# Attention value products in quarters of the matmul array, and first pairs loaded in runs of four tokens

## The chip, the cores and the metric

The kernel runs on one core of one Trainium2 chip. The metric is device time in microseconds (us). Before the change three runs took 802.65, 802.65 and 802.79 us; the median is 802.65.

## What is computed

Normalised attention on 8 batches, 12 heads, 448 tokens, 64 channels a head, and then a feed-forward block on the 3584 x 768 result:

```python
q_n, k_n = (rmsnorm(q, g_q), rmsnorm(k, g_k))
scores = scale * np.matmul(q_n, k_n.transpose(0, 1, 3, 2))
scores = scores - np.max(scores, axis=-1, keepdims=True)
attn = np.exp(scores)
attn = attn / (np.sum(attn, axis=-1, keepdims=True) + 1e-09)
attn_out = np.matmul(attn, v)
...
h = x @ w_in                      # 768 -> 1024
e = np.exp(h - np.max(h, axis=-1, keepdims=True))
solu = h * (e / (np.sum(e, axis=-1, keepdims=True) + 1e-09))
ln = (solu - mu) / np.sqrt(var + 1e-06) * g_ln
out = ln @ w_out                  # 1024 -> 768
```

## The kernel before

fast_path does all of it in three stages that follow each other on TensorE. general_path is another way for unusual inputs, and isn't run here.

**Attention.** The 96 heads are done four at a time: a "quad" m, 0 to 23, holds two "pairs" a = 2m and b = 2m + 1 of two heads each. A pair's normalised q and k lie transposed in a tile qkT, head h on partitions 64h to 64h + 63. `scores` (L812) multiplies 64 keys of one head at a time, so four matmuls use the four quarters (64 x 64) of the array, and writes one tile s of two PSUM banks; ScalarE takes the exponential (L802) into a tile E. Of 448 keys, three such units of 128 keys belong to each pair, and the last 64 keys of both pairs share a unit (`scores_last`, L825). A quad thus has seven score units. `values_last` (L858) starts the output o of both pairs from the last keys, in quarters; `values(a)` and `values(b)` (L869) add the other keys with all 128 rows and half the columns of the array. `sums` (L891) adds E over the keys with a matrix of ones, 32 columns at a time. `inverse` and `divide` (L902 to L918) turn the sums into factors and multiply o by them into xo; `store_x` (L926) puts xo into a scratch tensor xd in HBM.

The next quads are prepared alongside: `load` (L636), `squares` on ScalarE (L672), `row_sums` on VectorE (L680), `fold_sums` on Pool (L690, L691), `rsqrt_seed` on ScalarE (L697, L698, result ny), `normalise` on Pool (L713), `qk_transpose` on VectorE (L723) and `gain` on ScalarE (L727). `add` (L839) and `add_more` (L848) add E tiles into es ahead of the sums. In twelve quads, w_in is also converted from 64-bit words: `begin` and `step` on ScalarE and VectorE (L535 to L542), `combine_in` on Pool (L563).

The order of all this is written out by hand: the tile framework's scheduler is off (`tc.manual_schedule()`), every engine runs its instructions in the order in which the loop over m emits them, and the framework adds the waits for data and for buffers that come free. `unit(f)` emits a piece of TensorE's work and counts its steps; `later(n, f)` emits f after n more units. In the loop, a quad emits scores(a, 0), store_x(m - 1), the other score units with the preparation between them, then squares, gains and sums, then `outputs` (values_last and values(a)), the weight conversion, values(b), and the sums.

The first two pairs take another way: `load_rows` (L738) loads them with tokens on partitions, `square_rows`, `sum_rows` and `normalise_rows` (L772) work on rows, `transpose_rows` (L778) transposes q (s = 0) and k (s = 1) on TensorE into PSUM tiles pt, and `take_rows` (L784 to L788) copies these to qkT, on ScalarE for pair 0, on ScalarE and VectorE for pair 1.

**Hidden layer.** For each of 14 groups of 256 tokens `products` (L990) makes x @ w_in out of seven block products into PSUM banks A, B, C, D. `load_x` (L942) brings a group from xd; `sizes` (L951) squares it on ScalarE for a check at the end of the program; `block_sums` (L970 to L974) makes the sums of blocks on Pool; `plus` (L1006) adds a bank to an earlier part on VectorE. **Output.** `outer_product` (L1205) does the same for the second matrix.

## Time and profile before

The page shown is of one profiled execution. That execution took 803.36 us; the span from its first to its last instruction is 801.6 us.

| | |
|---|---|
| profiled execution | 803.36 us |
| its span | 801.6 us |
| median of the runs | 802.65 us |
| TensorE busy (PE) | 788.1 us, 98% |
| VectorE (DVE) | 613.7 us, 77% |
| Pool | 523.1 us, 65% |
| ScalarE (ACT) | 472.2 us, 59% |
| L812 scores / L869 values | 120.1 us / 113.8 us of TensorE |
| granted TensorE clock | 0.999 |

By stretch TensorE is busy 7.0 of the first 10.6 us, 21.9 of the next 22.9, all of 33.5 to 296.7, 18.6 of the 19.6 us to 316.3, and all of 316.3 to 560.

How to read the lines below. A timeline line has the start in us, the length, the engine, the line of the kernel, the operation, output and inputs, how many instructions were merged, and in brackets how long the engine sat idle before and what ended that. PE is TensorE's matmul; each fp32 matmul is two records (passes), so L869's 24 are 12 matmuls. Matmuls are pipelined: one begins before the one ahead has ended, and the spacing of the starts tells what one costs. A form such as 64*64 is the part of the array that is used, rows by columns. A line of the chain of waits has the start, the length, and the engine and line that the end of the program hung on at that time; "issue" is time without a visible cause.

### The profile page before, as it was taken

How to read it: one execution, taken by the hardware profiler on the slowest of the kernel's cores; microseconds unless marked ns; L12 is line 12 of the kernel's file. 1: busy time of each engine (PE TensorE's matmuls, PEld its weight loads, DVE VectorE, ACT ScalarE, POOL GpSimd, SP SyncE). 2: the span in 40 equal slices, each digit the busy share in tenths (PEclk: the TensorE clock that was granted, in tenths of full speed). 3: DMA queues.
4: the chain of work that ended last, by engine and by line, in shares of the span. 5: the costliest groups of instructions: out<-in, count | busy, mean ns of one | idle time of the engine just before them, and what ended most of it. 6: DMA issues, size and time to landing. Idle time of an engine off the chain costs nothing.

```text
span 801.6 us, 14271 instructions
## 1 busy us (share of the span) xinstructions
PE 788.1 (98%) x4854; PEld 462.7 (58%) x4854; DVE 613.7 (77%) x1202; ACT 472.2 (59%) x783; POOL 523.1 (65%) x664
## 2 busy tenths in 40 slices
PE   8999999999999999999999999999999999999997
PEld 4344444444444443444444444444789999999996
DVE  6787989989888896488878666777896776866945
ACT  6677878878778774376766544444515455464420
POOL 2666777778876784234456467668698777877861
PEclk9999999999999999999999999999999999999999
DMA  9878889897787832445554435552757457366312
GB/s 169 164 174 156 175 194 186 194 189 161 169 157 169 158 102 75 136 117 155 152 146 131 113 98 141 142 137 52 190 167 233 147 183 264 123 221 223 112 61 83
DMA packets 269598, 122.68 MB, mean 153 GB/s; under 512 B 187596, under 2 KB 254668, under 8 KB 269516
## 3 DMA queue, kind: packets, MB, share of 16 engines
q1 hardware_dynamic: 254332, 111.78, 55.9%
q10 hardware_dynamic: 15184, 9.90, 4.5%
q8 instruction: 40, 0.66, 0.3%
q14 instruction: 42, 0.34, 0.1%
HBM read 84.94 MB, written 36.70 MB: 152 GB/s over the span
## 4 chain that ended last, share of the span: by engine, by line
PE 87%; DVE 3%; DMA 2%; SPq 2%; POOL 2%; ACT 2%; issue 1%; DVEq 0%; ACTq 0%; POOLq 0%
PE A L1205 14%; PE A L990 13%; PE o L869 12%; PE s L812 12%; PE B L990 8%; PE B L1205 7%; PE C L990 4%; PE sm L891 4%; PE D L990 4%; PE C L1205 3%; PE s L825 2%; PE o L858 2%; SPq L636 1%; DMA xg<-xd 1%; ACT E L802 1%
## 5 line engine op out<-in xcount | busy, mean ns | idle before, releaser
L802 ACT ACTIVATE E<-s 128x896 f32<-128x896 f32 x168 | 138.8, 937 | 8.3 <-PE s L812 7.8
L812 PE MATMUL s<-qkT 64*64 64x448 f32 x1152 | 120.1, 545 | 1.0 <-ACT qkT L786 0.6
L869 PE MATMUL o<-E,v 128*64 128x448 f32 x576 | 113.8, 543 | 0.0
L1079 POOL TENSOR_TENSOR he<-he,mhalf 128x1 f32<-128x1 f32 x28 | 27.4, 977 | 102.5 <-DVE he L1078 97.4
L812 PEld LDWEIGHTS s<-qkT 64*64 64x64 f32 x1152 | 48.0, 163 | 59.4 <-ACT E L802 29.3
L1205 PE MATMUL A<-w_out,sums 128*128 128x192 f32 x392 | 79.9, 327 | 1.6 <-POOL sums L1185 1.2
L869 PEld LDWEIGHTS o<-E,v 128*64 128x64 f32 x576 | 39.1, 137 | 72.2 <-issue 68.0
L1205 PE MATMUL B<-w_out,sums 128*128 128x192 f32 x392 | 79.8, 326 | 0.5 <-DVE P L1267 0.5
L713 POOL TENSOR_TENSOR qkn<-qk,ny 128x896 f32<-128x896 f32 x46 | 77.2, 1699 | 3.8 <-DMA qk<-in_q_dram 1.5
L848 POOL TENSOR_TENSOR es<-es,E 128x896 f32<-128x896 f32 x22 | 46.4, 2110 | 48.8 <-ACT sq L672 34.0
L990 PE MATMUL B<-w_in,xsum 128*128 128x512 f32 x168 | 76.7, 592 | 0.0
L990 PE MATMUL A<-w_in,xg 128*128 128x512 f32 x168 | 74.6, 593 | 0.0
L1061 ACT ACTIVATE u<-h,hmax 128x1024 f32<-128x1024 f32 x28 | 32.2, 1148 | 66.8 <-DVE hmax L1055 66.8
L1205 PEld LDWEIGHTS A<-w_out,sums 128*128 128x128 f32 x392 | 66.1, 190 | 2.4 <-POOL sums L1185 1.5
L1205 PEld LDWEIGHTS B<-w_out,sums 128*128 128x128 f32 x392 | 66.2, 190 | 0.8 <-DVE P L1267 0.8
L839 DVE TENSOR_TENSOR es<-E 128x896 f32<-128x896 f32 x48 | 53.9, 1124 | 2.7 <-ACT E L802 2.7
L990 PEld LDWEIGHTS B<-w_in,xsum 128*128 128x128 f32 x168 | 31.9, 190 | 40.2 <-issue 39.2
L990 PEld LDWEIGHTS A<-w_in,xg 128*128 128x128 f32 x168 | 31.8, 190 | 40.1 <-issue 39.3
L690 POOL COPY ss<-part 32x56 f32<-32x56 f32 x92 | 47.0, 511 | 5.9 <-DVE part L680 1.4
L680 DVE TENSOR_REDUCE part<-sq 128x28 f32<-128x896 f32 x46 | 47.9, 1080 | 3.9 <-ACT sq L672 1.6
L723 DVE STREAM_TRANSPOSE qkT<-qkn 128x896 f32<-128x896 f32 x46 | 48.4, 1087 | 0.0
L563 POOL TENSOR_TENSOR w_out<-w_out 128x384 f32<-128x384 f32 x44 | 45.0, 1028 | 1.3
(153 smaller groups left out, 1651.0 us busy)
## 6 DMA issues: line engine op xcount, KB each, us to landing
ur<-ud SPq DMA_DIRECT2D x60, 256.0 KB, 4.6
ud<-ub SPq DMA_DIRECT2D x112, 128.0 KB, 2.3
xd<-xo SPq DMA_DIRECT2D x48, 224.0 KB, 3.0
qk<-in_q_dram SPq DMA_DIRECT2D x92, 112.0 KB, 3.1
qk<-in_k_dram SPq DMA_DIRECT2D x92, 112.0 KB, 3.0
v<-in_v_dram SPq DMA_DIRECT2D x24, 384.0 KB, 4.3
out_dram<-P SPq DMA_DIRECT2D x19, 384.0 KB, 4.2
raw<-in_moe_w_in_dram SPq DMA_DIRECT2D x12, 512.0 KB, 5.3
```

What stands on the lines that cost most here:

```text
L563: nc.gpsimd.tensor_tensor(o, p, q, OP.subtract)
L680: nc.vector.tensor_reduce(norms[m]["part"][:, i], st[n]["sq"], AX, OP.add)
L690: e.tensor_copy(ss[g * 32 : g * 32 + 32], part[o * 32 : o * 32 + 32])
L713: e.tensor_tensor(d["qkn"].rearrange("p (s b) d -> p s b d", s=2), d["qk"].rearrange("p s (b d) -> p s b d", d=32), y.rearrange("p (s b) - ...
L723: nc.vector.transpose(d["qkT"].rearrange("p s t -> p (s t)"), d["qkn"].rearrange("p b d -> p (b d)"))
L802: nc.scalar.activation(d["E", kc], s[:, :, 0:S], AF.Exp)
L812: nc.tensor.matmul(s[c : c + D, h, 0:S], d["qkT"][hh, 1, keys], d["qkT"][hh, 0, :], start=True, stop=True,)
L839: nc.vector.tensor_tensor(d["es"], d["E", 0], d["E", 1], OP.add)
L848: e.tensor_tensor(d["es"], d["es"], d["E", 2], OP.add)
L869: nc.tensor.matmul(d["o"][h * D : (h + 1) * D, :], quads[n // 2]["v"][:, n % 2 + 2 * h, kc], d["E", kc][:, h], start=False, stop=(kc == NJ ...
L990: nc.tensor.matmul(k[bank], a[:, c], w_in[i][:, c], start=begin and c == 0, stop=c == HD - 1, skip_group_check=not begin,)
L1205: nc.tensor.matmul(k[bank], a[:, c].rearrange("p a i -> p (a i)"), w_out[:, area, i, c], start=begin and c == 0, stop=c == KC - 1, skip_gr ...
```

## The change

- `load_rows` gives each partition four tokens in a row (1 KB) in place of single tokens of 256 bytes. `normalise_rows` writes its result, in another order, to the tile of the squares; `transpose_rows` takes it from there and writes every fourth column of PSUM. The two tiles pt become one tile of two banks.
- `values_part` replaces `values` in quads 1 to 22 ("halved"). It works in quarters of the array: half 0 takes rows 0 to 63 of pair a and rows 64 to 127 of pair b, half 1 the others. `turn` is an instruction without work on ScalarE that waits for half 0; half 1's first matmul waits for it. scores(a + 2, 0) of the next quad stands between the halves.
- o of both pairs is one tile of two banks, `divide` does both with one transpose and one product, and the banks B and D of `products` are one tile.
- gain(a + 2) goes ahead of the squares and gain(b + 2) behind the turn; sizes(0) goes from the end of quad 22 to quad 23, behind its last exponentials, and writes to another tile; the last pair's add_more goes from VectorE to Pool.

```diff
@@ -732,17 +732,17 @@
     def load_rows(n, queues):
         b, hp = divmod(n, NP)
         d = st[n] = {}
-        d["qk"] = xs.tile([P, 2, 4, P], FP32, tag="x", name="x")[0:R]
+        d["qk"] = xs.tile([P, 2, 2, 4, D], FP32, tag="x", name="x")[0:R]
         for s, src in enumerate((q, k)):
             for h in range(2):
                 queues[2 * s + h].dma_start(
-                    d["qk"][:, s, :, h * D : (h + 1) * D], src[b, 4 * (hp // 2) + hp % 2 + 2 * h].rearrange("(j p) d -> p j d", p=R)
+                    d["qk"][:, s, h], src[b, 4 * (hp // 2) + hp % 2 + 2 * h].rearrange("(p j) d -> p j d", p=R)
                 )
 
     def square_rows(n, s, engine):
         d = st[n]
         if s == 0:
-            d["sq"] = xs.tile([P, 2, 4, P], FP32, tag="x", name="xsq")[0:R]
+            d["sq"] = xs.tile([P, 2, 2, 4, D], FP32, tag="x", name="xsq")[0:R]
         x, y = d["qk"][:, s], d["sq"][:, s]
         if engine is nc.scalar:
             nc.scalar.activation(y, x, AF.Square)
@@ -754,28 +754,35 @@
         if s == 0:
             d["ss"] = small.tile([P, 4 * NB], FP32, tag="ss", name="ss", bufs=2)[0:R, 0:16]
         nc.vector.tensor_reduce(
-            d["ss"][:, s * 8 : s * 8 + 8], d["sq"][:, s].rearrange("p j (h d) -> p (j h) d", h=2), AX, OP.add
+            d["ss"][:, s * 8 : s * 8 + 8], d["sq"][:, s].rearrange("p h j d -> p (h j) d"), AX, OP.add
         )
 
     def warm_up():
 
         w = work.tile([P, 2, S], FP32, tag="r", name="warm", bufs=1)[:, 0]
         nc.vector.memset(w, 0.0)
-        o = ps_t.tile([P, S], FP32, tag="o", name="pt", bufs=2)
+        o = ps_t.tile([P, 2, 512], FP32, tag="o", name="pt", bufs=1)[:, 0, 0:S]
         for _ in range(5):
             nc.tensor.matmul(o, w[:, 0:P], w, start=True, stop=True)
 
+    def flat(x):
+        return x.rearrange("p h j d -> p (h j d)")
+
     def normalise_rows(n, s):
         d = st[n]
-        x = d["qk"][:, s].rearrange("p j (h d) -> p (j h) d", h=2)
-        y = d["y"][:, s * 8 : s * 8 + 8].rearrange("p i -> p i ()").to_broadcast([R, 8, D])
-        nc.vector.tensor_tensor(x, x, y, OP.mult)
+        y = d["y"][:, s * 8 : s * 8 + 8].rearrange("p (h j) -> p h j ()", h=2).to_broadcast([R, 2, 4, D])
+        o = flat(d["sq"][:, s]).rearrange("p (j h d) -> p h j d", h=2, d=D)
+        nc.vector.tensor_tensor(o, d["qk"][:, s], y, OP.mult)
 
     def transpose_rows(n, s):
         d = st[n]
-        d["pt", s] = ps_t.tile([P, S], FP32, tag="o", name="pt", bufs=2)
+        if s == 0:
+            d["pt"] = ps_t.tile([P, 2, 512], FP32, tag="o", name="pt", bufs=1)
+        d["pt", s] = d["pt"][:, s, 0:S]
         for j in range(4):
-            nc.tensor.transpose(d["pt", s][:, j * R : (j + 1) * R], d["qk"][:, s, j], ident[0:R, 0:R])
+            nc.tensor.transpose(
+                d["pt", s].rearrange("p (r j) -> p j r", j=4)[:, j], flat(d["sq"][:, s])[:, j * P : (j + 1) * P], ident[0:R, 0:R]
+            )
 
     def take_rows(n, s):
         d = st[n]
@@ -838,20 +845,24 @@
         d["es"] = work.tile([P, 2, S], FP32, tag="es", name="es")
         nc.vector.tensor_tensor(d["es"], d["E", 0], d["E", 1], OP.add)
 
+    def halved(m):
+        return 0 < m < NQ - 1
+
     def whole(n):
         return on_vector(n // 2) or n % 2 == 0
 
     def add_more(n):
         d = st[n]
         if whole(n):
-            e = nc.vector if on_vector(n // 2) else nc.gpsimd
+            e = nc.vector if on_vector(n // 2) and n < 2 * NQ - 1 else nc.gpsimd
             e.tensor_tensor(d["es"], d["es"], d["E", 2], OP.add)
 
     def values_last(m):
 
         d = quads[m]
+        o = d["o"] = ps_t.tile([P, 2, 512], FP32, tag="o", name="o", bufs=1)
         for i in range(2):
-            o = st[2 * m + i]["o"] = ps_t.tile([P, S], FP32, tag="o", name="o", bufs=2)
+            st[2 * m + i]["o"] = o[:, i, 0:S]
         for h in range(2):
             for i in range(2):
                 pp = slice(i * D, (i + 1) * D)
@@ -859,6 +870,36 @@
                     st[2 * m + i]["o"][h * D : (h + 1) * D, :], d["vl"][pp, h], d["E", NJ][pp, h],
                     start=True, stop=False,
                 )
+
+    def values_part(m, part):
+
+
+        first = None
+        for kc in range(NJ):
+            for i in range(2):
+                d = st[2 * m + i]
+                pp = slice((part ^ i) * D, (part ^ i) * D + D)
+                for h in range(2):
+                    x = nc.tensor.matmul(
+                        d["o"][h * D : (h + 1) * D, :], quads[m]["v"][pp, i + 2 * h, kc], d["E", kc][pp, h],
+                        start=False, stop=(part == 1 and kc == NJ - 1),
+                    )
+                    first = first or x
+        if part == 0:
+            quads[m]["half"] = x
+        else:
+            behind(first, quads[m]["turn"])
+
+    def behind(x, y):
+        tc.add_manual_dep(
+            getattr(x, "ins", x), getattr(y, "ins", y).name,
+            mybir.DependencyInfo(mybir.DependencyClass.Sync, mybir.DependencyReason.DATA),
+            reason="row tiles change banks",
+        )
+
+    def turn(m):
+        x = quads[m]["turn"] = nc.scalar.nop()
+        behind(x, quads[m]["half"])
 
     def values(n):
 
@@ -910,13 +951,13 @@
                 nc.gpsimd.tensor_copy(rc[o : o + 32, :, t], rc[a : a + 32, :, t])
 
     def divide(m):
-        xo = quads[m]["xo"] = work.tile([P, 2, S], FP32, tag="xo", name="xo", bufs=1)
+        d = quads[m]
+        xo = d["xo"] = work.tile([P, 2, S], FP32, tag="xo", name="xo", bufs=1)
+        r = work.tile([P, 2 * NB, 32], FP32, tag="r", name="r", bufs=1)
+        nc.vector.transpose(r, d["rc"].rearrange("p i t b -> p (i t b) ()").to_broadcast([P, 2 * NB, 32]))
+        nc.vector.tensor_tensor(xo, d["o"][:, :, 0:S], r.rearrange("d (i b) x -> d i (b x)", i=2), OP.mult)
         for i in range(2):
-            n = 2 * m + i
-            r = work.tile([P, NB, 32], FP32, tag="r", name="r", bufs=1)
-            nc.vector.transpose(r, quads[m]["rc"][:, i].rearrange("p t b -> p (t b) ()").to_broadcast([P, NB, 32]))
-            nc.vector.tensor_tensor(xo[:, i], st[n]["o"], r.rearrange("d b i -> d (b i)"), OP.mult)
-            del st[n]
+            del st[2 * m + i]
 
     def store_x(m):
         b, hp = divmod(2 * m, NP)
@@ -947,9 +988,12 @@
         x = gs[g, "x"].rearrange("p c t -> p (c t)")
         n = HD * 2 * P
         sm = gs[g, "s"] = xs.tile([P, 3, HD, P], FP32, tag="x", name="xsum")
+        y = sm.rearrange("p k c t -> p (k c t)")
+        if g == 0:
+            y = work.tile([P, 2 * NB, 32], FP32, tag="sq", name="sq", bufs=2).rearrange("p b d -> p (b d)")
         for i in range(2):
             nc.scalar.activation(
-                sm.rearrange("p k c t -> p (k c t)")[:, 0:n], x[:, i * n : (i + 1) * n], AF.Square,
+                y[:, 0:n], x[:, i * n : (i + 1) * n], AF.Square,
                 accum_out=xmax[:, 2 * g + i : 2 * g + i + 1],
             )
 
@@ -984,8 +1028,12 @@
             sm = gs[g, "s"]
             a = {"a11": a11, "a12": a12, "s3": a21, "a22": a22, "s1": sm[:, 0], "s2": sm[:, 1], "s4": sm[:, 2]}[a]
             if begin:
-                tag = "t" if bank in "AC" or bank == "B" and g == NG - 1 else "o"
-                k[bank] = ps_t.tile([P, 512], FP32, tag=tag, name=bank, bufs=3 if tag == "t" else 2)[:, 0:n]
+                if bank in "AC" or bank == "B" and g == NG - 1:
+                    k[bank] = ps_t.tile([P, 512], FP32, tag="t", name=bank, bufs=3)[:, 0:n]
+                else:
+                    if "BD" not in k:
+                        k["BD"] = ps_t.tile([P, 2, 512], FP32, tag="o", name="BD", bufs=1)
+                    k[bank] = k["BD"][:, "BD".index(bank), 0:n]
             for c in range(HD):
                 nc.tensor.matmul(
                     k[bank], a[:, c], w_in[i][:, c],
@@ -1387,7 +1435,10 @@
 
             def outputs():
                 values_last(m)
-                values(a)
+                if halved(m):
+                    values_part(m, 0)
+                else:
+                    values(a)
 
 
             next1 = m + 1 < NQ
@@ -1446,15 +1497,18 @@
                 load_v(m + 1)
             if m == 1:
                 load(m + 3)
-            unit(lambda: scores(a, 0))
             if m == 1:
+                unit(lambda: scores(a, 0))
                 gain(3)
+            else:
+                unit(lambda: scores(a, 1))
             store_x(m - 1)
             if early:
                 qk_transpose(a + 2)
                 if next3 and m > 1:
                     load(m + 3)
-            unit(lambda: scores(a, 1))
+            if m == 1:
+                unit(lambda: scores(a, 1))
             unit(lambda: scores(a, 2))
             unit(lambda: scores_last(m))
             unit(lambda: scores(b, 0))
@@ -1465,13 +1519,14 @@
             if not on_vector(m):
                 add_more(a)
             unit(lambda: scores(b, 2))
+            if not next1:
+                sizes(0)
+            if next1:
+                gain(a + 2)
             if next2:
                 squares(a + 4)
                 squares(b + 4)
                 row_sums(a + 4)
-            if next1:
-                gain(a + 2)
-                gain(b + 2)
             if next2:
                 row_sums(b + 4)
                 fold_sums(m + 2)
@@ -1480,6 +1535,9 @@
                 add_more(a)
                 add_more(b)
             unit(outputs)
+            if halved(m):
+                turn(m)
+                gain(b + 2)
             step(m - 2)
             begin(m)
             step(m - 1)
@@ -1490,7 +1548,11 @@
                 load_next()
             if m == 3:
                 norm_gain()
-            unit(lambda: values(b))
+            if halved(m):
+                unit(lambda: scores(a + 2, 0))
+                unit(lambda: values_part(m, 1))
+            else:
+                unit(lambda: values(b))
             if m == NQ - 1:
                 block_sums(0, 0)
                 block_sums(0, 1)
@@ -1501,7 +1563,6 @@
                 later(1, lambda m=m: divide(m))
             if m == NQ - 2:
                 load_x(0)
-                sizes(0)
         divide(NQ - 1)
         store_x(NQ - 1)
         first.close()
```

## The prediction

> **What bounds the kernel now.** I read the page first: the chain that ended last is TensorE for 87%, and its busy row is at 9 tenths in all slices but the first and the last. So time can change only where TensorE waits or where its own stream gets shorter. I then read TensorE's timeline for one turn of the quad loop (four heads; 24 turns, m = 0 to 23):
>
> ```profile
> 120.51 0.93 PE L858 MATMUL o<-E,vl 64*64 64x448 f32 x8
> 121.37 4.73 PE L869 MATMUL o<-E,v 128*64 128x448 f32 x24
> 126.03 0.96 PE L891 MATMUL sm<-E,ones 128*32 128x224 f32 x16
> 126.82 0.94 PE L891 MATMUL sm<-es,ones 128*32 128x224 f32 x16
> 127.69 2.52 PE L812 MATMUL s<-qkT 64*64 64x448 f32 x24
> 130.03 0.93 PE L825 MATMUL s<-qkT 64*64 64x448 f32 x8
> 130.78 2.43 PE L812 MATMUL s<-qkT 64*64 64x448 f32 x24
> 133.03 0.93 PE L858 MATMUL o<-E,vl 64*64 64x448 f32 x8
> ```
>
> Read the starts, not the durations. L825 to the second L812 is 0.75 us for eight 64*64 passes: four run at once and a group of four starts every 376 ns. From such starts in the trace a 128*64 pair also takes 376 ns, a 128*32 group of four 189 ns. Without a break a quad is 16 x 0.376 + 12 x 0.376 + 8 x 0.189 = 12.04 us; the period (120.51 to 133.03) is 12.52. The other 0.48 us is at changes of tile shape: into L869 the first start is 109 ns late and the second 51 (160 ns); into L891 100 + 24; back into L812 114 + 84. There is no other wait between 40 and 296 us, but for 0.3 us in one quad that holds the transpose of the norm's gain.
>
> ScalarE in the same stretch, which the change hangs a new wait on:
>
> ```profile
> 121.85 1.84 ACT L672 ACTIVATE sq<-qk 128x896 f32<-128x896 f32 x2
> 123.53 1.27 ACT L727 ACTIVATE qkT<-qkT,gcol 128x448 f32<-128x448 f32 x2
> ...
> 128.11 0.34 ACT L697 ACTIVATE ny<-ss,eps 128x56 f32<-128x56 f32 x1 [1.98 <-POOL ss L691]
> 128.48 0.25 ACT L698 ACTIVATE ny<-ny 128x56 f32<-128x56 f32 x1
> 128.77 5.78 ACT L802 ACTIVATE E<-s 128x896 f32<-128x896 f32 x7
> 134.37 1.01 ACT L672 ACTIVATE sq<-qk 128x896 f32<-128x896 f32 x1
> ```
>
> Call TensorE's first score T0 (127.69). The exponentials start at T0 + 1.08, one every 0.80, the squares at T0 + 6.68.
>
> Two places outside the steady part carry waits. At the chain's end of the attention:
>
> ```profile
> 296.34 7.09 DMA xg<-xd
> ...
> 305.17 0.19 ACT xsum L951
> 305.36 0.81 ACT E L802
> 306.17 0.04 issue
> 306.21 0.98 PE s L825 x8
> ```
>
> ScalarE sits in sizes(0) until a load lands, and the last quad's exponentials are queued behind it. And at the start:
>
> ```profile
> 13.03 0.98 PE L778 MATMUL pt<-ident,x 112*128 112x112 f32 x8
> ...
> 14.05 0.62 DVE L788 COPY qkT<-pt 128x448 f32<-128x448 f32 x1 [0.50 <-PE pt L778]
> 14.07 0.65 ACT L784 ACTIVATE qkT<-pt,gcol 128x448 f32<-128x448 f32 x1
> ```
>
> All eight transposes of pair 1 run together and VectorE and ScalarE take the two halves side by side.
>
> **Quarters in place of L869, quads 1 to 22.** 24 passes of 128*64 become 48 of 64*64. By the rows they cost the same: L858 accumulates in the same four quarters at 376 ns per four, so 12 x 0.376 = 4.51 us both ways. The Trainium skill speaks against splitting ("TensorEngine Tiling (Array Packing)", Instruction Overhead): it gives each matmul about 60 cycles. If that came on top, the 24 extra passes of each quad, four at once, would cost 6 x 25 ns = 0.15 us (25 ns being 60 cycles at the 2.4 GHz the skill's first page gives), and the gain below would be gone. The row has four passes of 448 columns in 376 ns with nothing between them, so I take 0. What falls away is the change of shape from L858: 160 ns. The change into L891 stays, now from 64*64: no row shows that pair; the three that are there cost 124, 160 and 198 ns. I take 109 + 24 = 133, near the 124 of the same target. Saved: 160 + 124 - 133 = 0.151 us a quad, 22 x 0.151 = **-3.3 us** (bounds 0.09 to 0.18 a quad: -2.0 to -4.0).
>
> **The new wait between the halves.** The second half's row tiles write the other bank, so the built program puts a wait on ScalarE's sequencer (after gain(a+2) and both squares) for the end of half 0, and half 1 waits for it. Between stand the next quad's scores(a+2, 0), 0.75 us. Times from T0: six exponentials to 5.88, gain to 6.52, squares to 8.36. TensorE: six score units and the change to 4.60, L858 to 5.35, half 0 to 7.60 (its last pass ends at 7.77), scores to 8.36. Half 1 wants to start at 8.36. The sequencer runs ahead of the datapath: at 283.55 to 283.74 the chain has ScalarE's sequencer handling the squares' waits before the last exponential begins at 283.78. So the wait should be passed at about 7.85, 0.5 us early: 0. Behind it queue gain(b+2), the weight conversion and the next exponential; the second square covers the sequencer until 8.36. Conversion quads have less room: Pool's sums end at T0 + 0.39, the seed at 1.05, the exponential at 1.08. The squares move 0.16 us earlier (one exponential of 0.80 leaves, one gain of 0.64 comes before), the period shrinks by 0.15, so the loop just holds. I allow **+0.2** (0 to 1.5).
>
> **Divide in one piece.** 2 x 0.65 (L917) + 2 x 0.62 (L918) becomes one transpose (1.09 by the L723 row of that size) and one product (about 1.12 by L839), 0.3 us less on VectorE, which is not on the path. It must end before L858 reuses the banks: T0 + 4.25 against 4.60. The cover is 0.35 us; what is late beyond that is paid by TensorE. I take 0.
>
> **The last quad.** sizes(0), 2 x (0.84 + 0.19) us of ScalarE, goes behind the last exponential; nothing needs its result before the final check. In the steady quads L858 starts 5.34 us after T0, in the last one 6.79 (302.68 to 309.47): **-1.45** (-1.0 to -1.6). add_more(b) goes from VectorE to Pool (2.1 us by L848), done by about T0 + 8.5; the sums want it at 10.5. It pushes Pool's block_sums from T0 + 4.6 to 8.5, done at 14.3; the product that wants them starts near 16.8. Both 0, with 2 us of cover.
>
> **The two banks as one tile: products B and D.** The built program now makes D's first matmul wait for VectorE's read of B, which stood in another tile before. At 11 of the 13 places that read ends 0.7 to 1.1 us before D. At two it doesn't:
>
> ```profile
> 367.39 0.69 DVE L1006 CUSTOM_DVE_ANT_0 h<-B,u 128x512 f32<-128x512 f32 x1 [2.01 <-ACT u L997]
> 367.87 2.31 PE L990 MATMUL D<-w_in,xg 128*128 128x512 f32 x5
> ```
>
> D would start at about 368.28 (read-out 0.08, signal and weight load 0.1): 0.4 us. At 421.94 likewise 0.5. This stage has no slack, so **+0.9** (0 to 1.8, if other places slip too).
>
> **The start.** Rows of 1 KB instead of 256 B. Before, 1,792 packets carry pair 0, from 1.77 to 3.82 us. In this trace a 1 KB packet takes 57 ns (mean of 6,144), so 448 of them on 16 engines take 1.6 us: 0.45 earlier. The skill ("DMA: Bandwidth & Descriptors", Specifications) has full rate from 512 B on and about 27 GiB/s an engine: 35 ns, 1.0 us, so 1.05 earlier. I take the row, -0.45 (bounds -0.25 to -1.05). Writing every fourth PSUM column: the trace has no strided transpose; the four of one half take 0.49 us, between 0 and 0.5 more per half, and I take 0 since the stream in is the same.
> But pt is now one tile for both halves, and the built program waits by the tile. Pair 0: the first take waits for both transposes: 9.44 becomes about 10.0, +0.55, so scores start at 10.7 instead of 10.58. Pair 1: half 1's transposes wait until ScalarE has taken half 0, which stands behind three exponentials: 14.24 to 14.89, transposes to 15.46, VectorE's copy 15.52 instead of 14.05: +1.45. From there the chain has no slack: es, two row sums, Pool's es (15.83 to 17.93) and copies, ny at 20.35, squares, Pool's sums at 27.27, E, L825 at 28.77, after which TensorE no longer waits. Value: **+1.4** (bounds -0.5 to +1.8).
>
> **Sum.** -3.3 + 0.2 - 1.45 + 0.9 + 1.4 = -2.25 us. The profiled execution took 803.36 us (span 801.6 and 1.8 around it): 801.1. The median of the timed runs lies 0.7 below it: **800.4**.
>
> **Rivals.**
> Start free: the chain's slack or a faster load swallows the wait by the tile, and D never waits. -3.3 - 1.45 + 0.2: 798.1. For it: the load of quad 2 and the issues of SP run into the same stretch and come earlier; against it: the built waits. 0.17.
> The loop of Pool and ScalarE takes the gain in the twelve conversion quads (seed at 1.05 against 1.08): these keep 12.52, ten quads gain 1.5, the other terms stand: 802.0, no change. 0.15 (0.02 of it slower).
> Slower: half 1 waits in every quad. It decides if ScalarE's sequencer doesn't pass the wait until the second square is done, at 8.36: signal 0.1 and weight load 0.14 then stand bare, 0.25 x 22 = +5.5: 805.7. Place: the first pass of half 1, after the inserted score unit. For it: six exponentials, a gain and two squares stand ahead of the wait on ScalarE; against it: the sequencer rows at 283.55. 0.13.
> Forecast: 0.55.
>
> **Numbers.** 0.2%, 1.6 us, is about what a measurement here can tell from no change. The forecast's own range, 798.6 to 802.3 (the bounds together, not all at one end), lies mostly below 801.0; I count six in seven of it as faster: 0.47 + 0.17 = 0.64. Same: 0.08 + 0.13 = 0.21; slower 0.13 + 0.02 = 0.15. The range leaves most of the slow rival out: 797.6 to 803.4.
>
> **What would show it.** L858 to the quarters without the 109 + 51 ns, period 12.37 from 40 us on; the next quad's exponential between the halves; no idle time into half 1. L825 of the last quad at T0 + 1.6 with no ScalarE wait ahead. Two waits of TensorE on VectorE before D. At the start, half 1's transposes of pair 1 after ScalarE's take, and continuous TensorE from about 30.2 instead of 28.77. I am wrong if the period isn't 12.37, or if the start comes earlier.

## The result, and the profile after

Over 18 runs each, on the same chips, the kernel before has a median of 803.34 us and the changed kernel 801.95 us (801.10 to 803.03): a ratio of 0.9982 with a 95% interval of 0.9975 to 0.9988. That is 1.4 us faster, at the bound of 0.2% between "faster" and "no change". The profiled execution took 802.04 us (span 800.2) instead of 803.36 (801.6).

Lines of the changed kernel have new numbers: scores L819, scores_last L832, values_last L869, values_part L883, values L910, sums L932, exponentials L809, the takes L791 to L795, products L1038, plus L1054, the output's matmuls L1253.

Where the time went, from the starts of TensorE's matmuls in the traces (us); the last two columns are of experiments told below:

| | before | changed | tiles split | split, norm moved |
|---|---|---|---|---|
| first value matmul of quad 1 | 32.58 | 34.06 | 32.20 | 32.33 |
| period of a steady quad | 12.52 | 12.37 | 12.37 | 12.37 |
| period before the last quad | 13.71 | 12.22 | 12.24 | 12.23 |
| first product of the hidden layer | 316.26 | 313.21 | 311.37 | 311.48 |
| hidden layer, first to last start | 252.02 | 252.89 | 252.05 | 252.05 |
| first output matmul to the end of the span | 232.84 | 233.70 | 233.32 | 232.73 |
| span | 801.6 | 800.2 | 797.2 | 796.7 |

The steady quad on TensorE in the changed kernel:

```profile
121.06 0.93 PE L869 MATMUL o<-E,vl 64*64 64x448 f32 x8
121.82 2.44 PE L883 MATMUL o<-E,v 64*64 64x448 f32 x24
124.07 0.93 PE L819 MATMUL s<-qkT 64*64 64x448 f32 x8
124.82 2.44 PE L883 MATMUL o<-E,v 64*64 64x448 f32 x24
127.19 0.96 PE L932 MATMUL sm<-E,ones 128*32 128x224 f32 x16
...
133.43 0.93 PE L869 MATMUL o<-E,vl 64*64 64x448 f32 x8
```

From 121.06 to 121.82 is 0.76 us for eight quarter passes: the late start into the values is gone. The second half starts 0.75 us after the inserted scores, with no idle time in brackets, and 133.43 - 121.06 is 12.37 us.

ScalarE in that stretch:

```profile
119.97 2.56 ACT L809 ACTIVATE E<-s 128x896 f32<-128x896 f32 x3
122.36 0.71 ACT L727 ACTIVATE qkT<-qkT,gcol 128x448 f32<-128x448 f32 x1
122.92 1.83 ACT L672 ACTIVATE sq<-qk 128x896 f32<-128x896 f32 x2
124.60 0.71 ACT L727 ACTIVATE qkT<-qkT,gcol 128x448 f32<-128x448 f32 x1
```

The gain behind the turn starts at 124.60, as the squares end. The weights of half 1, which wait for the turn, are loaded before that:

```profile
124.07 0.18 PEld L819 LDWEIGHTS s<-qkT 64*64 64x64 f32 x4 [0.19 <-issue]
124.45 0.15 PEld L883 LDWEIGHTS o<-E,v 64*64 64x64 f32 x4 [0.19 <-issue]
124.82 0.15 PEld L883 LDWEIGHTS o<-E,v 64*64 64x64 f32 x4 [0.22 <-issue]
```

PEld is TensorE's weight load. The first load of half 1, at 124.45, keeps the spacing of its neighbours, so the turn was passed while the second square still ran (to 124.75).

The last quad, ScalarE first and TensorE second:

```profile
305.32 2.56 ACT L809 ACTIVATE E<-s 128x896 f32<-128x896 f32 x3
307.71 0.89 ACT L995 ACTIVATE sq<-xg 128x768 f32<-128x768 f32 x1
```

```profile
303.41 0.93 PE L832 MATMUL s<-qkT 64*64 64x448 f32 x8
304.16 2.44 PE L819 MATMUL s<-qkT 64*64 64x448 f32 x24
306.42 0.93 PE L869 MATMUL o<-E,vl 64*64 64x448 f32 x8
```

The squares of the token group stand behind the exponentials now, and no bracket of TensorE names ScalarE. The start and the first of the two late D products, from the timeline:

```profile
13.22 0.60 PE L783 MATMUL pt<-ident,xsq 112*128 112x112 f32 x4
14.26 0.65 ACT L791 ACTIVATE qkT<-pt,gcol 128x448 f32<-128x448 f32 x1
14.96 0.60 PE L783 MATMUL pt<-ident,xsq 112*128 112x112 f32 x4 [1.14 <-ACT qkT L791]
15.67 0.62 DVE L795 COPY qkT<-pt 128x448 f32<-128x448 f32 x1 [2.00 <-PE pt L783]
...
364.35 0.69 DVE L1054 CUSTOM_DVE_ANT_0 h<-BD,u 128x512 f32<-128x512 f32 x1 [2.02 <-ACT u L1045]
364.96 0.08 DVE L1054 DVE_READ_ACCUMULATOR2_ANT top<- 128x1 f32 x1
...
365.10 1.12 PE L1038 MATMUL BD<-w_in,xg 128*128 128x512 f32 x2
```

TensorE sits idle 1.14 us until ScalarE has read the other half of pt, and VectorE's copy comes at 15.67 instead of 14.05. D's first matmul at 365.10 stands behind VectorE's read of B; the start ahead of it is 709 ns earlier, instead of some 430, and the next start follows after 533 ns, another 0.1 us late. The other such gap, at 419.6, is 783 ns, again with 0.1 us more behind it.

### The profile page after: what moved, and what is told of

The parts are those of the page before. It is cut to its first block, busy times and chain, and to the rows that moved or that the text cites. A ratio compares the mean times of both kernels' runs of the same rounds, so it can differ in the third digit from the quotient of the medians.

```text
span 800.2 us, 15287 instructions
## 1 busy us (share of the span) xinstructions
PE 786.5 (98%) x5382; PEld 469.2 (59%) x5382; DVE 609.2 (76%) x1153; ACT 473.3 (59%) x783; POOL 524.3 (66%) x665
## 4 chain that ended last, share of the span: by engine, by line
PE 88%; DVE 4%; POOL 2%; SPq 1%; ACT 1%; DMA 1%; issue 1%; DVEq 0%; ACTq 0%; POOLq 0%
PE A L1253 14%; PE s L819 13%; PE o L883 12%; PE BD L1038 12%; PE A L1038 12%; PE B L1253 7%; PE sm L932 5%; PE C L1038 5%; PE C L1253 3%; PE s L832 2%; PE o L869 2%; SPq L636 1%; PE o L910 1%; DMA ur<-ud 0%; DVE ub L1142 0%
## 5 line engine op out<-in xcount | busy, mean ns | idle before, releaser
L809 ACT ACTIVATE E<-s 128x896 f32<-128x896 f32 x168 | 141.4, 933 | 12.8 <-PE s L819 11.6
L819 PE MATMUL s<-qkT 64*64 64x448 f32 x1152 | 124.0, 544 | 1.6 <-ACT qkT L793 1.2
L883 PE MATMUL o<-E,v 64*64 64x448 f32 x1056 | 107.2, 536 | 0.0
L819 PEld LDWEIGHTS s<-qkT 64*64 64x64 f32 x1152 | 49.8, 163 | 58.2 <-issue 25.2
L858 POOL TENSOR_TENSOR es<-es,E 128x896 f32<-128x896 f32 x23 | 49.1, 2135 | 51.4 <-DVE es L846 51.4
L1253 PE MATMUL A<-w_out,sums 128*128 128x192 f32 x392 | 80.1, 327 | 2.2 <-POOL sums L1233 1.3
L1253 PE MATMUL B<-w_out,sums 128*128 128x192 f32 x392 | 79.9, 326 | 0.4 <-DVE P L1315 0.4
L1038 PE MATMUL A<-w_in,xg 128*128 128x512 f32 x168 | 74.6, 593 | 0.0
L883 PEld LDWEIGHTS o<-E,v 64*64 64x64 f32 x1056 | 40.6, 133 | 58.0 <-issue 58.0
L1038 PE MATMUL BD<-w_in,xsum 128*128 128x512 f32 x156 | 71.2, 592 | 0.0
L1253 PEld LDWEIGHTS A<-w_out,sums 128*128 128x128 f32 x392 | 66.1, 190 | 3.3 <-POOL sums L1233 1.6
L1253 PEld LDWEIGHTS B<-w_out,sums 128*128 128x128 f32 x392 | 66.3, 190 | 0.8 <-DVE P L1315 0.7
L846 DVE TENSOR_TENSOR es<-E 128x896 f32<-128x896 f32 x48 | 56.9, 1189 | 0.7 <-ACT E L809 0.7
L1038 PEld LDWEIGHTS A<-w_in,xg 128*128 128x128 f32 x168 | 31.8, 190 | 40.1 <-issue 39.3
L723 DVE STREAM_TRANSPOSE qkT<-qkn 128x896 f32<-128x896 f32 x46 | 50.9, 1106 | 4.1 <-POOL qkn L713 4.1
L1038 PEld LDWEIGHTS BD<-w_in,xsum 128*128 128x128 f32 x156 | 29.5, 190 | 37.5 <-issue 35.2
L1253 PE MATMUL A<-w_out,s 128*128 128x192 f32 x224 | 45.7, 326 | 0.0
```

Source lines behind the costliest of these rows:

```text
L723: nc.vector.transpose(d["qkT"].rearrange("p s t -> p (s t)"), d["qkn"].rearrange("p b d -> p (b d)"))
L809: nc.scalar.activation(d["E", kc], s[:, :, 0:S], AF.Exp)
L819: nc.tensor.matmul(s[c : c + D, h, 0:S], d["qkT"][hh, 1, keys], d["qkT"][hh, 0, :], start=True, stop=True,)
L846: nc.vector.tensor_tensor(d["es"], d["E", 0], d["E", 1], OP.add)
L858: e.tensor_tensor(d["es"], d["es"], d["E", 2], OP.add)
L883: x = nc.tensor.matmul(d["o"][h * D : (h + 1) * D, :], quads[m]["v"][pp, i + 2 * h, kc], d["E", kc][pp, h], start=False, stop=(part == 1 a ...
```

## Experiments

Twelve runs were made, one of them of the changed kernel once more; each ratio is to the kernel before on the same chip. The changed kernel itself was 0.9982, and 0.9984 in its second comparison.

### The two-bank tiles, both and one by one

The first kernel gives pt, and B and D, separate tiles of one bank; o stays one tile. Since the two banks are used in turn, each use has a PSUM pool of its own that is closed before the next (the pools' bookkeeping is left out here). The second and third kernels do one half of it each.

```diff
...
-        if s == 0:
-            d["pt"] = ps_t.tile([P, 2, 512], FP32, tag="o", name="pt", bufs=1)
-        d["pt", s] = d["pt"][:, s, 0:S]
+        d["pt", s] = two("rows").tile([P, 512], FP32, tag=f"p{s}", name="pt")[:, 0:S]
...
-                    if "BD" not in k:
-                        k["BD"] = ps_t.tile([P, 2, 512], FP32, tag="o", name="BD", bufs=1)
-                    k[bank] = k["BD"][:, "BD".index(bank), 0:n]
+                    banks_two("products")
+                    k[bank] = two("products").tile([P, 512], FP32, tag=bank, name=bank)[:, 0:n]
```

> The two PSUM banks that the change made into one tile for the rows of the first pairs (pt) and for the products B and D are given back as two tiles of one bank each; the values' sums (o) stay one tile of two banks. Theory (the joined tiles couple the two banks: a reader of one bank holds the writer of the other): quad 1's first value matmul comes at 32.1 to 32.4 us instead of 34.06, the two gaps of 709 and 783 ns in the hidden stage (at 365.1 and 419.6 us) go, and the time falls by 1.7 to 2.0 plus 0.87 us, to about 799.3 us in the profiled execution and 0.9950 of the kernel before. Rival 1 (the lead at the start is given back later, at a transfer that doesn't move): only the 0.87 us, 0.9972. Rival 2 (the late copies come from the strided columns of PSUM, not from the tile): the same, 0.9972 or nearer to 0.9982. If the 0.86 us that the output stage had grown by is also a consequence of the stalls in the hidden stage, it goes too: 0.9940.

Measured: median 798.84 us, ratio 0.9944 (0.9931 to 0.9958). Quad 1 at 32.20, hidden stage 252.05. Both parts of the theory hold.

> Only the rows of the first pairs (pt) are given back two tiles of one bank; B and D stay one tile. Theory: quad 1's first value matmul at 32.1 to 32.4 us instead of 34.06, the whole rest of the kernel earlier by as much: 0.9958 to 0.9962 of the kernel before (802.04 to about 800.2 us profiled). Rival (the lead is given back at a transfer or in another engine's queue before quad 4): 0.9982, with a longer period in quads 1 to 3. Rival (strided columns of PSUM make the copies late): no earlier start, 0.9982. The output stage tells whether its added 0.86 us is there whatever happens at the start.

Measured: 799.56 us, 0.9953 (0.9939 to 0.9966). Quad 1 comes at 32.14, and the lead of 1.92 us is still there at the first product (311.29 against 313.21). The start in this kernel's timeline:

```profile
12.62 0.98 PE L795 MATMUL pt<-ident,xsq 112*128 112x112 f32 x8
13.53 1.47 PE L844 MATMUL s<-qkT 64*64 64x448 f32 x6
13.64 0.62 DVE L807 COPY qkT<-pt 128x448 f32<-128x448 f32 x1 [0.55 <-PE pt L795]
13.65 0.65 ACT L803 ACTIVATE qkT<-pt,gcol 128x448 f32<-128x448 f32 x1
```

The eight transposes are one group again and the two copies run side by side, with the strided columns of PSUM still in place. So the columns are not what made the copies late: the shared tile is. Pair 0's part is 0.60 us (first scores at 10.17 instead of 10.77), pair 1's the other 1.32.

> Only B and D are given back two tiles of one bank; the rows of the first pairs stay one tile. Theory: the gaps of 709 and 783 ns in the hidden stage go, the stage takes 252.0 us instead of 252.9, and the time falls by 0.87 us: 0.9971 of the kernel before. Rival (the matmuls that wait for VectorE would be held by something else a moment later): stage 252.9, 0.9982. If the output stage's added 0.86 us came from ScalarE being late at the end of the hidden stage because of these stalls, the output stage is 232.8 instead of 233.7 us and the ratio is 0.9960; if that is spread from run to run or has another cause, it stays between 232.8 and 233.7 and doesn't follow this edit.

Measured: 801.10 us, 0.9977 (0.9968 to 0.9985). The stage takes 252.05 us. At the first of the two places this kernel's timeline has:

```profile
364.34 0.69 DVE L1068 CUSTOM_DVE_ANT_0 h<-B,u 128x512 f32<-128x512 f32 x1 [2.01 <-ACT u L1059]
364.81 1.45 PE L1052 MATMUL D<-w_in,xg 128*128 128x512 f32 x3
```

D starts while VectorE still reads B. The output stage is 233.11 us, between the two values, which the expectation had put down to spread or another cause; that stage is taken up below.

### The squares of the first token group put back

```diff
-            if not next1:
-                sizes(0)
...
             if m == NQ - 2:
                 load_x(0)
+                sizes(0)
```

> The squares of the first token group (sizes) are put back to where they were, the end of the last quad but one; all else as in the changed kernel, the last pair's addition on GpSimd among it. Theory (the two squares of 1.4 us or so in ScalarE's queue ahead of the last quad's exponentials made its period 13.71 us): the last period is 13.6 to 13.7 instead of 12.22 us, time +1.45 us: 1.0000 of the kernel before. Rival (the period fell because the last pair's addition went from VectorE to GpSimd): last period stays at 12.2 to 12.4, 0.9982.

Measured: 801.95 us, 0.9987 (0.9980 to 0.9993), but the profiled execution has a last period of 16.14 us. It was run again.

> The kernel with the squares of the first token group put back behind the last quad but one, once more. In its first profile PE idled 1.94 us in the last quad, its granted clock was 0.64 and 0.50 for the 4 us after, and the last period was 16.14 us; the median of its runs was only 0.05% above the changed kernel's. Theory (the wait is there in each execution, the halved clock only in some): last period 13.7 to 14.2 us without a lowered clock. Rival (the clock falls in each execution): 16.1 us again. The time against the kernel before: 0.9987 again if the output stage is shorter by about as much as the last quad is longer, 1.0000 if not.

Measured: 802.74 us, 0.9997 (0.9988 to 1.0005); last period 14.02 us. TensorE's line in the first of the two profiles, and the windows there (stretch and length, busy time of TensorE, its weight loads, VectorE, ScalarE and Pool with their counts, then the granted clock, DMA's share and GB/s):

```profile
306.33 4.21 PE L819 MATMUL s<-qkT 64*64 64x448 f32 x24 [1.94 <-ACT E L809]
```

```profile
304.00:306.00 2.00, 0.39 (x6) 0.00 (x0) 1.97 (x2) 1.97 (x5) 1.92 (x2) 1.00 0.00 0
306.00:308.00 2.00, 1.67 (x12) 0.73 (x16) 1.23 (x2) 1.89 (x3) 0.51 (x1) 0.64 0.31 70
308.00:310.00 2.00, 2.00 (x15) 0.55 (x10) 0.00 (x0) 1.40 (x2) 0.00 (x0) 0.50 0.82 198
```

and TensorE in the second:

```profile
305.67 2.63 PE L819 MATMUL s<-qkT 64*64 64x448 f32 x24 [1.44 <-ACT E L809]
```

In both, TensorE waits for an exponential that is queued behind the squares, so the place of sizes is what the last quad's period hangs on, and not the addition that went to Pool, which is on Pool in both. In the first profile the idle 1.94 us were followed by half the clock, in the second 1.44 us by none of that (1.00 in all windows). By the ratios the two are only 0.3 and 1.1 us slower than the changed kernel, less than the 1.8 us of the period; the output stage gave back 1.2 to 1.3 us in the first of these profiles (232.37 us against 233.57 and 233.70), and 0.1 to 0.2 in the second (233.49). What makes up the rest is open.

### The values as before

values(a) and values(b) over all 128 rows in all quads, and the order of scores and gains that goes with them (their lines in the loop are left out):

```diff
     def halved(m):
-        return 0 < m < NQ - 1
+        return False
...
```

> The values are computed as in the kernel before (128x64 passes over all 128 keys, pair a and then pair b, the two gains in ScalarE's queue ahead of them, each quad's first scores at its own start); the loads, the joined tiles, the place of sizes and of the last addition are those of the changed kernel. Theory (22 quads lose 0.15 us each by the quarters): period 12.52 us again, time +3.3 us, about 805.3 us profiled, 1.0022 of the kernel before. Rival 1 (the quarters gained nothing and the shorter period comes from the merged division or the gains' place): period 12.37, 0.998. Rival 2 (the whole values are held by the one-tile o, whose division of two banks ends later): period over 12.6 us, 1.005 or more.

Measured: 804.79 us, 1.0027 (1.0017 to 1.0037). TensorE in this kernel:

```profile
121.93 0.93 PE L869 MATMUL o<-E,vl 64*64 64x448 f32 x8
122.79 4.73 PE L910 MATMUL o<-E,v 128*64 128x448 f32 x24
127.45 0.96 PE L932 MATMUL sm<-E,ones 128*32 128x224 f32 x16
...
134.45 0.93 PE L869 MATMUL o<-E,vl 64*64 64x448 f32 x8
```

The period is 12.52 us with the merged division and the one tile o in place: what the quarters bring is the 0.15 us of the shape changes, and nothing else of the loop contributes. The period before the last quad is 12.22 us here too: in quad 22 the quarters bring nothing.

### The turn without its cover

```diff
-                unit(lambda: scores(a + 2, 0))
                 unit(lambda: values_part(m, 1))
+                unit(lambda: scores(a + 2, 0))
```

> The next quad's first scores are put behind the second half of the values, so that the second half follows the first with nothing between them but the wait for the turn on ScalarE. Theory (the four score passes are the cover of that wait): PE idles 0.3 to 0.5 us ahead of the second half in each of 22 quads, the period is 12.7 to 12.9 us, time +7 to +11 us over the changed kernel, 1.007 to 1.012 of the kernel before. Rival 1 (half 1's wait costs nothing even bare): 12.37 us, 0.998. Rival 2 (the next quad's first exponentials come 2.4 us later and ScalarE becomes the bound): period over 13 us and idle PE ahead of the scores or the values' first pass, 1.02 or more.

Measured: 809.16 us, 1.0085 (1.0067 to 1.0104), period 12.73 us. From the waits of this kernel (total us, times, longest) and its timeline:

```profile
PEld o L883 <- ACTq L901: 19.1, 21, 0.9
```

```profile
123.92 5.05 PE L883 MATMUL o<-E,v 64*64 64x448 f32 x48
128.79 0.93 PE L819 MATMUL s<-qkT 64*64 64x448 f32 x8
```

48 quarter passes take 4.87 us instead of 2 x 2.25: 0.36 us a quad is the bare wait, and the inserted scores hide all of it. The row of the waits tells who: the weight load waits for ScalarE's sequencer in 21 quads (its 0.9 us are longer than the 0.36, since the passes ahead still run while the load waits).

### The rows of the first pairs as before

```diff
-                    d["qk"][:, s, h], src[b, 4 * (hp // 2) + hp % 2 + 2 * h].rearrange("(p j) d -> p j d", p=R)
+                    d["qk"][:, s, :, h * D : (h + 1) * D], src[b, 4 * (hp // 2) + hp % 2 + 2 * h].rearrange("(j p) d -> p j d", p=R)
...
-                d["pt", s].rearrange("p (r j) -> p j r", j=4)[:, j], flat(d["sq"][:, s])[:, j * P : (j + 1) * P], ident[0:R, 0:R]
+                d["pt", s][:, j * R : (j + 1) * R], d["qk"][:, s, j], ident[0:R, 0:R]
```

> The first pairs are loaded in single tokens (packets of 256 bytes), normalised in place and transposed into 112 neighbouring columns as in the kernel before; the PSUM tile of two banks, and all else, is that of the changed kernel. Theory (the load in runs of four saves 0.45 us, the strided columns cost nothing, the lateness is the joined tile's): first squares at 4.57 instead of 4.12 us, quad 1's first value matmul at 34.4 to 34.6 instead of 34.06, +0.45 us, 0.9988 of the kernel before. Rival (the strided columns of PSUM make the transposes or ScalarE's copies slower): quad 1's first value matmul at 34.0 or less, 0.998 or less. A third outcome is that the earlier landing is taken up by a wait on another engine at the start (the copy of the gain column, at 8.27 us in the changed kernel): no difference.

Measured: 802.41 us, 0.9998 (0.9989 to 1.0007). First squares at 4.55 instead of 4.12 us, quad 1 at 34.40 instead of 34.06: the longer rows are worth 0.43 us at the landing and 0.34 at quad 1 (the profiles that share the changed start have 33.95 to 34.09 there). The time says slower by more than that, but its interval reaches down to 0.9989.

### The output stage

> The changed kernel once more, unchanged, to see what differs between two executions of one program: 0.998 of the kernel before. If the output stage (first output matmul to the end of the span) is again 233.7 us and its first 112 matmuls again take 21.1 us, the added 0.86 us belongs to the program; if it lies elsewhere between 232.4 and 233.7 us, it is what the landing of transfers gives from one execution to the next. The attention loop and the hidden stage (252.9 us, two gaps over 700 ns) should repeat to within 0.05 us.

Measured: 801.56 us, 0.9984 (0.9977 to 0.9990). Loop and hidden stage repeat to 0.04 us, and so does the output's beginning: 112 matmuls in 21.11 us (21.10 in the first profile; 20.51 in the kernel before). An early gap there is 893 ns, before the fourth product, where TensorE waits for the copy q (L1265) on ScalarE. The next kernel moves the normalisation behind that copy:

```diff
-                (NG - 2, 1): (1, 2, 3, 5, 5), (NG - 2, 0): (1, 2, 4, 6, 7),
+                (NG - 2, 1): (1, 2, 3, 5, 5), (NG - 2, 0): (1, 2, 4, 6.25, 7),
```

> The changed kernel with one instruction of ScalarE's queue moved: the last normalisation of the hidden stage (L1133, 1.23 us) that stood ahead of the copy of the first output sum (q, L1265) stands behind it. Theory (the gap of 0.89 us at 1.8 us into the output stage is PE waiting for that copy, and it is the larger part of the output stage's 0.86 us): the gap is about 0.3 us, the first 392 output matmuls take 67.3 instead of 67.8 us, the output stage 233.1 instead of 233.7, time -0.5 us: 0.9977 of the kernel before. Rival (the next waits, at 13 and 32 us, take it up): the gap goes and the first 392 output matmuls take 67.8 us all the same, 0.9983.

Measured: 801.63 us, 0.9982 (0.9976 to 0.9988). The gap is gone and 112 matmuls take 21.09 us all the same: the theory of that gap fell. A wait later in the stage takes up all of it, as the rival had it. In the changed kernel's timeline it is this one:

```profile
566.49 2.51 POOL L1216 TENSOR_TENSOR s<-s,a 128x512 f32<-128x512 f32 x2
...
579.76 0.72 POOL L1232 TENSOR_TENSOR sums<-sums,a 128x256 f32<-128x256 f32 x1
579.85 1.18 DVE L1220 TENSOR_TENSOR s<-a,s 128x512 f32<-128x512 f32 x1
580.44 1.17 POOL L1233 TENSOR_TENSOR sums<-a 128x256 f32<-128x256 f32 x1
...
581.22 0.34 DVE L1267 TENSOR_TENSOR u<-A,P 128x192 f32<-128x192 f32 x1
...
581.71 0.89 PE L1253 MATMUL A<-w_out,sums 128*128 128x192 f32 x4 [1.31 <-POOL sums L1233]
```

The bracket names Pool's L1233, which came last. It can't be what TensorE waits for: the sum that this product reads is that of L1232, done at 580.48, and in the last kernel below the product starts before L1233 has ended. What ends the wait is VectorE's L1267, which reads a tile A: in all 14 profiles the product starts 0.14 or 0.15 us after it ends (581.56 to 581.71 here). L1267 stands in VectorE's queue behind the addition L1220, and L1220 meets Pool's L1232. Before:

```profile
568.07 2.52 POOL L1168 TENSOR_TENSOR s<-s,a 128x512 f32<-128x512 f32 x2
...
582.81 0.34 DVE L1219 TENSOR_TENSOR u<-A,P 128x192 f32<-128x192 f32 x1
...
583.30 0.89 PE L1205 MATMUL A<-w_out,sums 128*128 128x192 f32 x4 [1.22 <-POOL sums L1185]
```

The first output matmul comes at 568.72 before and at 566.54 after. So Pool's first addition of this stage (566.49 in the changed kernel, 568.07 before) starts 0.65 us ahead of it before, 0.05 after. In ten of the 14 profiles, before and after among them, VectorE's L1220 ends 0.54 or 0.55 us after Pool's L1232 (lines of the changed kernel), whenever it started; in these ten the time of the 112 matmuls is 21.14 to 21.16 us if it is counted from the start of Pool's first addition. There the length of the stretch is set by Pool, by way of VectorE, and not by TensorE. For the other four it is 20.34 to 20.58 us.

> Both splits of the two-bank tiles (rows of the first pairs; B and D) and the normalisation behind the copy of q. If the effects add: the two-tile version's 0.9944 and 0.4 us less for the output stage, 0.9939 of the kernel before, 796.8 us or so of span. Rival (the output stage takes it up): 0.9944.

Measured: 798.72 us, 0.9951 (0.9938 to 0.9964), not to be told from the 0.9944 of the split alone. Its span is 0.47 us shorter, but this profile is one of the other four.

> The changed kernel with one instruction without work at the head of ScalarE's queue and one at the head of VectorE's. In the traces so far the last ScalarE copy of the hidden stage starts 4.60 us before the first output matmul where it is the queue's record number 831, and 4.89 us before where it is 830, 811 or 807; VectorE's hsum starts 0.26 to 0.30 us late where it is record number 959 and at once where it is 958 or 1008. Theory (the delay belongs to the place in the queue, not to the work): with both moved on by one, the copy starts at -4.89, hsum at -2.15, GpSimd's first addition at -0.65 us instead of -0.05, and the first 112 output matmuls take 20.5 us instead of 21.1 (or 19.7 to 20.0 if VectorE's addition comes ahead of GpSimd's at 13 us), all as in the kernel before; time -0.6 us, 0.9976 of the kernel before. Rival (the delay comes from what happens on the engines then): -4.60, -1.59 and 21.1 us as in the changed kernel, 0.9983.

Measured: 801.26 us, 0.9978 (0.9971 to 0.9986). The instructions without work left no record in the trace and the record numbers are the same, so whether they took a place in the queue is not known, and the theory stays untested. Copy, hsum and Pool start as in the changed kernel (-4.60, -1.59, -0.05), and yet the 112 matmuls take 20.29 us. The profile shows why:

```profile
579.48 0.64 DVE L1220 TENSOR_TENSOR s<-a,s 128x512 f32<-128x512 f32 x1
579.64 1.07 POOL L1232 TENSOR_TENSOR sums<-sums,a 128x256 f32<-128x256 f32 x1
...
580.31 0.34 DVE L1267 TENSOR_TENSOR u<-A,P 128x192 f32<-128x192 f32 x1
...
580.67 0.72 POOL L1233 TENSOR_TENSOR sums<-a 128x256 f32<-128x256 f32 x1
580.79 0.89 PE L1253 MATMUL A<-w_out,sums 128*128 128x192 f32 x4 [0.78 <-POOL sums L1232]
```

Here VectorE's addition comes first and takes 0.64 us; in the changed kernel's profile Pool's comes 0.09 us ahead and VectorE's takes 1.18. VectorE's L1267 then ends at 580.65, and TensorE is released 0.8 us earlier against the first output matmul, while L1233 still runs. Which of the two is first differs between executions of one program: of the two profiles with sizes put back, VectorE's is first in one (112 matmuls in 20.02 us) and Pool's in the other (20.79 us).

## Why the prediction was right, and what it missed

The forecast was 800.4 us, the range 797.6 to 803.4; the median is 801.95. The direction and the mechanisms hold; the size was too hopeful by 1.55 us. By the prediction's own line of 0.2%, 1.6 us, the 1.4 us are no clear "faster": it had given that 0.64 and "same" 0.21, and the interval lies on both sides of the line. The median also stands beside the 802.0 of the rival in which Pool and ScalarE take the gain in the conversion quads; only the periods tell that it isn't that one.

- **The quarters**, 0.151 us a quad: 12.518 to 12.367 us a quad, and back to 12.52 in the kernel with whole values. The packing held: no price per matmul appeared for the 24 extra passes. Not all of the 22 quads gained it, though: quads 1 to 3 gained 0.10 to 0.12 us, and quad 22 nothing. Together it is 3.04 us instead of 3.3.
- **The turn**, 0.2 us allowed: it costs nothing, and 0.36 us a quad where its cover is taken away. That the 0.2 wasn't needed made up for what the quarters fell short of, by luck. The slower rival said 0.25 us a quad would stand bare; it had the right mechanism and a price near the measured one, but ScalarE's sequencer passes the wait in time. The loop rival (conversion quads keep 12.52) is wrong: 12.37 in nearly all quads; the first three of the 22 periods are 12.41, 12.42 and 12.71, the last of these with the transpose of the norm's gain.
- **The last quad**, -1.45: the period fell by 1.49, and went to 14.02 (once 16.14) when sizes was put back.
- **B and D**, +0.9 at two places: 0.87, exactly at the two. **The start**, +1.4: 1.48; within it the load -0.45 (measured 0.43 at the landing), pair 0's wait by the tile +0.55 (0.60), and all of it together +1.45 at pair 1's copy on VectorE (1.62: 14.05 to 15.67). The rival of a free start, 798.1 us, is what the kernel with split tiles shows to be there for the taking.

To the first output matmul the sum was -2.25 and the traces have -2.18 (568.72 to 566.54). Two terms failed.

**The output stage was not in the sum at all**, as though it would follow unchanged: it grew by 0.86 us. Of this 0.6 us comes from Pool's queue starting later against TensorE; the rest, 0.3 us, lies at the end of the span, where the profiles of all kernels differ by about as much (the time behind the first 392 output matmuls is 165.6 to 166.0 us).

That Pool starts later comes from two small delays ahead of it: ScalarE's last copy of the hidden stage starts 0.29 us later against the first output matmul, though its wait is over at the same time in both (4.95 us ahead), and VectorE's hsum another 0.3 us later. What makes them is open. Neither follows B and D. In all 14 profiles each is present or absent alike where its instruction has the same record number in its queue (831 with, 830, 811 and 807 without; 959 with, 958 and 1008 without). hsum has 958, and is in time, in just the three kernels that split the rows' tile; there the instruction behind it (he), now 959, starts 0.20 us late. That fits a delay that belongs to the place, but no run here tested it.

**The step from the profiled execution to the median**, -0.7 us, rested on three runs of before; over 18 runs before's median (803.34) is its profiled time (803.36), and the changed kernel's lies 0.09 below its own. 0.9 and 0.6 us make up the miss.

The kernel with split tiles beats both: 0.9944, some 3 us under the changed kernel. Moving the normalisation adds nothing that can be measured.

## What to carry to other kernels

When two buffers become one tile, list who reads one part while another writes the other part: here that cost 1.9 us at the start and 0.84 us later (252.89 against 252.05), and giving one use of the banks a joint tile and the others separate ones kept the gain without the price. A wait that is laid between two halves of a group needs independent work of its length between them, and 0.75 us of scores covered 0.36. Before a stage is taken as unchanged, ask which engine it hangs on at its beginning and what that engine's head start is: Pool's shrank from 0.65 to 0.05 us here, though nothing in that stage was edited. And where a bracket names an engine, compare a run that starts before that engine is done: in the output stage the name was the wrong one.

## What was not expected of the hardware

- **An idle TensorE can be followed by half the clock, or not.** After 1.94 us of waiting the granted clock was 0.64 and 0.50 in the next two stretches of 2 us; after 1.44 us, in another run of the same kernel and at the same place, 1.00. The Trainium skill ("TensorE: Matmul & The Clock Gate", Part 1) has the clock fall after an idle window of some 3.4 us. Here less sufficed, and the measurement decides.
- **Two additions of VectorE and Pool that meet are a race, and the loser pays.** VectorE's L1220 of 512 columns takes 0.64 or 0.65 us when it is first, and when Pool's L1232 is under way it ends 0.54 or 0.55 us after that one (1.18 us long in the changed kernel); Pool's takes 0.72 or 0.73 when first and 1.06 to 1.28 otherwise. The Trainium skill ("Trainium Architecture — The Big Picture", What this means for kernel authors) calls the port that they share an exclusive lock, and these rows agree. That 0.8 us of TensorE's time hangs on it is what only the traces show. The starts don't tell who wins when they are close: Pool's won with a start 0.09 us ahead in the changed kernel, and lost (1.28 us) with one 0.05 us ahead in the kernel that splits only B and D.
